# Tables of 32 channels built in place by two chains of VectorE operations, and the inverse's first step placed beside the taps

## The chip, the cores and the metric

The kernel runs on one core of a Trainium2 chip. It uses TensorE (PE in the profile, its weight loads are PEld), VectorE (DVE), ScalarE (ACT), very little of GpSimd (POOL), and SyncE (SP), whose queue issues nearly all transfers. The metric is the device time of one execution in microseconds (us). Three runs of the kernel before gave 597.43, 596.15 and 597.5 us, with a median of 597.43 us. Every engine works through its own list of instructions strictly in order. An instruction that is not ready holds back everything behind it on its engine.

## The reference, cut to what matters

Two independent computations stand side by side in the output.

```python
# A: Fourier mixing, x is 2048 x 512
a = einsum("bsd,ed->bse", x, dft_hid_re); b = einsum("bsd,ed->bse", x, dft_hid_im)
y_A = einsum("ts,bse->bte", dft_seq_re, a) - einsum("ts,bse->bte", dft_seq_im, b)

# B: S4D convolution, u is 2048 x 512, 128 modes for each of the 512 channels
dt = exp(log_dt); A = -exp(log_A_real) + 1j * A_imag; C = (C_real + 1j * C_imag) * dt[:, None]
K = 2.0 * einsum("dn,dnl->dl", C, exp((A * dt[:, None])[:, :, None] * arange(L))).real   # the taps
y_B = irfft(rfft(u_t, 2 * L) * rfft(K, 2 * L))[:, :, :L] + u * D_skip
return concatenate([y_A, y_B], axis=-1)
```

## The kernel before, in words

**Part A** (class `Fnet`) is a stream of 128x128 by 128x512 matrix products, line 273. Each factor is split into a high and a low part of the type fp32r, and each product is three matmuls: high by high, high by low, low by high. The split is done in `split` (lines 177 to 183): ACT rounds the high part (line 181) and DVE subtracts it (line 183). One item of the stream is one split tile, used by twelve matmuls. There are 160 items: 128 in the first eight groups (`s`) and 32 in the last four (`p`).

**Part B** (class `Ssm`) works on the 512 channels in 16 chunks of 32 channels (`CHUNK`). For every chunk it makes powers of a complex number, in which 2048 positions are written as 32 times 64. The seeds of a chunk are computed by `seed_args` (lines 532 to 536 on DVE, 528 to 546 on ACT) and multiplied into `cs` by `seeds` (line 556). From `cs` two tables are built by doubling. Table t1 has 32 columns per channel and table t2 has 64. A doubling is `mul` (line 482, into the scratch tiles `prod` or `prod2`), followed by `add` (line 491), which sums the halves of the scratch tile into the table. The even columns of t2 come from squares: `square` on ACT (line 500), `even_im` (line 508) and `even_re` (line 514) on DVE.

In the kernel before, the first columns of both tables are made for the 32 channels of a chunk at once in `base1` and `base2`. Then, for each half chunk of 16 channels, ACT copies the base into a fresh pair of tables t1 and t2 (`base_copy`, lines 652 and 654), and DVE makes the last two doublings for these 16 channels. The order in which the loop in `tables` (lines 607 to 648) yields its operations alternates between the two tables. There are three buffers of t1 and three of t2, each for 16 channels.

`taps` (lines 672 to 691) multiplies t1 by t2 on PE for two half chunks in one visit of 128 small matmuls (line 685), into one of the two slots `f` of PSUM. Each slot is two banks. `banks(n)` hands out n slots, and requests are served in the order in which they come. Two visits of taps give 64 channels, and `stage1_k` (line 705) starts their Fourier transform. Four quarters of 128 channels then go through `product` (lines 815 to 879): PE brings both spectra to frequency (line 826), ACT copies them out (line 839), four DVE operations multiply them (lines 842 to 855), and PE takes the first step of the inverse (line 862), which needs both slots. `inverse` (lines 890 to 911) loads the result back from memory and does the last step (line 901), ACT copies it out (line 906) and SP stores it (line 910).

**The order of the work** is made before launch, by the class `Plan` in the kernel file. Every piece of work is a generator that asks for an engine with a duration and an urgency. The planner takes, for the engine that comes free, the request that can start first and, among equals, the one with the smallest urgency number. The durations are formulas, such as 62 cycles plus one cycle per column for a DVE operation (`dve`, line 147). The matmuls of the stream have urgency 5, and all PE work of part B has urgency 1, so on PE the stream fills what part B leaves free. On DVE a split has urgency 0 while fewer than three items are ready ahead of the matmuls, the products of part B have 1 and the tables 2. What the planner decides is then the fixed order of each engine's list. If an engine is later on the chip than the planner thought, the order does not change and the others wait.

## Time and profile before

| what | value |
|---|---|
| median of three runs | 597.43 us |
| the profiled execution's own time | 599.18 us |
| its span, first to last instruction | 597.4 us |
| PE busy | 586.1 us (98%) |
| DVE busy | 504.7 us (84%) |
| ACT busy | 408.7 us (68%) |
| DMA queues, share of 16 engines | 69.3% |
| granted TensorE clock | 0.999 |

Busy time is the union of the instructions of an engine. Idle time in a row of the profile is the time that the engine stood still just before the instructions of that row, and the name behind the arrow is what ended most of it. The timeline lists instructions by engine with start, duration and shape; "x2" means that two like instructions were merged into one row. For PE it is best to compare starts: the end of a matmul is modelled, and consecutive matmuls overlap in the rows.

### The profile page before, as it was taken

How to read it: one execution, taken by the hardware profiler on the slowest of the kernel's cores; microseconds unless marked ns; L12 is line 12 of the kernel's file. 1: busy time of each engine (PE TensorE's matmuls, PEld its weight loads, DVE VectorE, ACT ScalarE, POOL GpSimd, SP SyncE). 2: the span in 40 equal slices, each digit the busy share in tenths (PEclk: the TensorE clock that was granted, in tenths of full speed). 3: DMA queues.
4: the chain of work that ended last, by engine and by line, in shares of the span. 5: the costliest groups of instructions: out<-in, count | busy, mean ns of one | idle time of the engine just before them, and what ended most of it. 6: DMA issues, size and time to landing. Idle time of an engine off the chain costs nothing.

```text
span 597.4 us, 17145 instructions
## 1 busy us (share of the span) xinstructions
PE 586.1 (98%) x6982; PEld 448.1 (75%) x6982; DVE 504.7 (84%) x993; ACT 408.7 (68%) x824; POOL 3.0 (0%) x12
## 2 busy tenths in 40 slices
PE   8999999999999999999999999999999999999997
PEld 6866666787867777887877877877778777787775
DVE  6999899989999999999999998999999996125540
ACT  5658898867767769677786686687867854344633
POOL 0000000000000000000000000000000000000000
PEclk9999999999999999999999999999999999999999
DMA  7998978472677656754856864568669637799756
GB/s 269 279 357 307 319 268 286 135 205 73 166 212 199 182 129 191 222 174 109 251 168 177 229 187 125 177 174 275 198 192 268 212 108 234 212 268 293 232 140 232
DMA packets 140991, 125.98 MB, mean 211 GB/s; under 512 B 46192, under 2 KB 105840, under 8 KB 140656
## 3 DMA queue, kind: packets, MB, share of 16 engines
q1 hardware_dynamic: 140912, 124.88, 69.3%
q8 instruction: 55, 0.90, 0.6%
q14 instruction: 24, 0.20, 0.1%
HBM read 82.12 MB, written 42.73 MB: 209 GB/s over the span
## 4 chain that ended last, share of the span: by engine, by line
PE 51%; DVE 25%; ACT 8%; DMA 7%; issue 7%; SPq 2%; DVEq 0%; ACTq 0%
PE acc L273 38%; DVE prod L482 7%; DVE lo L183 5%; DVE t L491 3%; PE f L826 3%; DMA par<-par_dram 3%; PE f L685 3%; PE f L901 2%; DMA raw<-in_sT 2%; PE f L862 2%; DVE base L491 2%; PE f L705 2%; ACT L540 2%; ACT hi L181 1%; DMA zl<-zs 1%
## 5 line engine op out<-in xcount | busy, mean ns | idle before, releaser
L273 PE MATMUL acc<-hi,x_hi 128*128 128x512 f32 x640 | 258.3, 404 | 0.5 <-ACT hi L181 0.3
L273 PE MATMUL acc<-lo,x_hi 128*128 128x512 f32 x640 | 250.8, 392 | 3.4 <-DVE lo L183 3.3
L273 PE MATMUL acc<-hi,x_lo 128*128 128x512 f32 x640 | 249.6, 390 | 0.0
L273 PEld LDWEIGHTS acc<-hi,x_hi 128*128 128x128 f32 x640 | 120.1, 188 | 49.7 <-issue 23.0
L183 DVE TENSOR_TENSOR lo<-raw,hi 128x512 fp32r<-128x512 f32 x160 | 109.6, 686 | 47.4 <-ACT hi L181 38.1
L273 PEld LDWEIGHTS acc<-lo,x_hi 128*128 128x128 f32 x640 | 120.2, 188 | 29.6 <-DVE lo L183 7.2
L273 PEld LDWEIGHTS acc<-hi,x_lo 128*128 128x128 f32 x640 | 120.2, 188 | 25.7
L181 ACT ACTIVATE hi<-raw 128x512 fp32r<-128x512 f32 x160 | 99.7, 626 | 58.0 <-PE acc L273 50.3
L482 DVE TENSOR_TENSOR prod<-base,cs 128x512 f32<-128x512 f32 (+3 forms) x160 | 88.9, 588 | 11.1 <-ACT base L593 9.2
L482 DVE TENSOR_TENSOR prod<-t,cs 128x1024 f32<-128x1024 f32 x64 | 78.1, 1221 | 0.8
L491 DVE TENSOR_TENSOR t<-prod 128x512 f32<-128x512 f32 (+1 forms) x128 | 68.1, 552 | 0.0
L287 ACT ACTIVATE y<-acc 128x512 f32<-128x512 f32 x48 | 28.3, 595 | 15.1 <-PE acc L273 13.0
L839 ACT ACTIVATE uk<-f 128x1024 f32<-128x1024 f32 x32 | 32.2, 1016 | 5.4 <-PE f L826 5.4
L685 PEld LDWEIGHTS f<-t,t 128*32 128x32 f32 x2048 | 29.5, 110 | 6.4 <-issue 3.5
L685 PE MATMUL f<-t,t 128*32 128x64 f32 x2048 | 32.3, 220 | 0.4 <-DVE t L491 0.4
L491 DVE TENSOR_TENSOR base<-prod 128x64 f32<-128x64 f32 (+2 forms) x96 | 28.8, 337 | 0.0
L842 DVE TENSOR_TENSOR z<-uk 128x512 f32<-128x512 f32 x32 | 22.0, 687 | 7.4 <-ACT uk L839 7.4
L500 ACT ACTIVATE prod<-t 128x512 f32<-128x512 f32 x32 | 20.1, 627 | 11.8 <-DVE t L491 11.7
L586 ACT ACTIVATE cs<-cs 128x352 f32<-128x352 f32 x32 | 15.3, 527 | 15.8 <-DVE cs L556 15.8
L500 ACT ACTIVATE square<-base 128x256 f32<-128x256 f32 x48 | 19.6, 408 | 5.2 <-DVE base L491 5.2
L714 ACT ACTIVATE xk_sb<-f 128x512 f32<-128x512 f32 x32 | 17.6, 595 | 7.8 <-PE f L705 7.8
L869 ACT ACTIVATE z<-f 128x512 f32<-128x512 f32 x32 | 17.7, 590 | 7.4 <-PE f L862 7.4
(90 smaller groups left out, 552.8 us busy)
## 6 DMA issues: line engine op xcount, KB each, us to landing
raw<-in_sT SPq DMA_DIRECT2D x128, 256.0 KB, 3.3
p<-y SPq DMA_DIRECT2D x32, 256.0 KB, 4.0
xt_u<-xu SPq DMA_DIRECT2D x32, 256.0 KB, 5.1
xk<-xk_sb SPq DMA_DIRECT2D x32, 256.0 KB, 3.9
xt_k<-xk SPq DMA_DIRECT2D x32, 256.0 KB, 5.3
zs<-z SPq DMA_DIRECT2D x32, 256.0 KB, 3.8
zl<-zs SPq DMA_DIRECT2D x16, 512.0 KB, 5.1
raw<-p SPq DMA_DIRECT2D x32, 256.0 KB, 3.7
```

Source lines behind the costliest of these rows:

```text
L181: self.nc.scalar.activation(hi, src, AF.Copy)
L183: self.nc.vector.tensor_tensor(lo, src, hi.bitcast(F32), op=OP.subtract)
L273: nc.tensor.matmul(acc[d], l[:, cols], r, start=k == 0 and n == 0, stop=k == len(items) - 1 and n == 2)
L287: self.nc.scalar.activation(y, ps, AF.Copy, scale=-1.0 if g[2] == 1 else 1.0)
L482: self.nc.vector.tensor_tensor(p.rearrange("p k d c m -> p k (d c) m"), src.rearrange("p d c l -> p (d c) l")[:, None, :, rows].to_broadca ...
L491: self.nc.vector.tensor_tensor(dst[:, :, :, rows], p[:, 0], p[:, 1, :, ::-1], op=OP.add)
L500: self.nc.scalar.activation(sq, t[:, :, :, m // 2:m], AF.Square)
L685: nc.tensor.matmul(ps[32 * j:32 * j + 32, 4 * o + i], t1[:, 4 * i + j, c], t2[:, 4 * i + j, c], start=c == 0, stop=c == 1, tile_position=( ...
L826: nc.tensor.matmul(got[r][1][32 * xx:32 * xx + 32, g, o:o + PART], self.w2[rows, 2 * q + r, xx, 32 * c:32 * c + 32], xt[rows, r, xx], star ...
L839: a.activation(uk[:, r].rearrange("p g n c d -> p g (n c d)"), p, AF.Copy)
L842: v.tensor_tensor(P[:, r], t[:, r], u[:, r], op=OP.mult)
L869: a.activation(z[:, :, 2 * n:2 * n + 2].rearrange("p r x d -> p x r d"), p[:, :, :2 * PART].rearrange("p x (r d) -> p x r d", r=2), AF.Copy)
```

## The change

In part B the two tables of a chunk are made for all 32 channels in their final tiles. There is no base tile and no copy by ACT. `tables` now only makes the seeds, in two buffers of `cs`. Two new generators consume them: `tables2` builds t2 (urgency 2, scratch `prod2`, one buffer of t2), and `tables1` builds t1 (urgency 2.2, scratch `prod`, two buffers of t1). Only the last doubling is still done in two halves of 16 channels, because of the size of the scratch tile.

`taps` now takes one chunk from one pair of tables and writes it to columns 256 to 511 of the two banks of a slot. The first step of the inverse in `product` writes only columns 0 to 255 of each bank. As long as taps are left to do, a product that has come this far waits in a list (class `Joined`). The next visit of taps takes it along: it asks for two slots instead of one, issues the inverse's 32 matmuls and then its own 128, and the first slot is given back when both have been copied out. A product that finds no taps left goes alone, as before.

Three smaller edits go along. At the start, the first 128 columns of the first tile of x are loaded and split on their own (`load_x0`), the first tile of the moving factor is loaded by ACT's queue instead of SP's, and the three warming matmuls have 216 columns instead of 256. At the end, the last of the inverse's steps is copied out in two halves by ACT and DVE and stored by two queues.

```diff
     def load(self, src, to, where, key, ev):
         raw = self.pool.tile([128, DM], F32, name="raw", bufs=RAWS)
-        yield "dma", load(256)
-        self.nc.sync.dma_start(raw, src)
+        if key == self.items[self.groups[0]][0]:
+            yield "act", 0.45
+            self.nc.scalar.dma_start(raw, src)
+            yield "dma2", load(256)
+        else:
+            yield "dma", load(256)
+            self.nc.sync.dma_start(raw, src)
...
+    def load_x0(self, raw):
+        yield "dma", load(64)
+        self.nc.sync.dma_start(raw[:, :128], self.xin[0, :, :128])
+        self.x[0] = self.still(0)
+        yield "act", act(128)
+        self.nc.scalar.activation(self.x[0][0][:, :128], raw[:, :128], AF.Copy)
+        yield "dve", dve(128)
+        self.nc.vector.tensor_tensor(self.x[0][1][:, :128], raw[:, :128], self.x[0][0][:, :128].bitcast(F32),
+                                     op=OP.subtract)
+        self.plan.set(self.x0_ev)
...
+class Joined(Event):
+    def __init__(self, ssm, run):
+        super().__init__()
+        self.ssm, self.fn, self.got = ssm, run, None
+    def run(self, got, shared=True):
+        self.got, self.users = got, {k: 1 for k, _ in got}
+        if shared:
+            self.users[got[0][0]] = 2
+        self.fn(got)
+    def leave(self, k):
+        self.users[k] -= 1
+        if not self.users[k]:
+            self.ssm.give(k)
...
+    def halves(self, name, t, rows, seed, to):
+        for d in (slice(0, CHUNK // 2), slice(CHUNK // 2, CHUNK)):
+            p = yield from self.mul(name, t[:, d], rows, seed[:, :, d])
+            yield from self.add(p, t[:, d], to)
+
+    def tables1(self):
+        for n in range(16):
+            yield self.t1s
+            yield self.cs_ev[n]
+            cs = self.cs[n]
+            t = self.tab.tile([128, CHUNK, 2, 32], F32, name="t1", bufs=2)
...
+            for j in range(4):
+                p = yield from self.mul("prod", t, slice(0, 2 ** j), cs[:, :, 6 + j])
+                yield from self.add(p, t, slice(2 ** j, 2 * 2 ** j))
+            yield from self.halves("prod", t, slice(0, 16), cs[:, :, 10], slice(16, 32))
...
+    def tables2(self):
+        for n in range(16):
+            yield self.cs_ev[n]
+            yield self.t2s
+            cs, t = self.cs[n], self.t2
...
+            p = yield from self.mul("prod2", t, slice(1, 2), cs[:, :, 1])
+            yield from self.add(p, t, slice(3, 4))
+            p = yield from self.mul("prod2", t, slice(1, 4), cs[:, :, 2])
+            yield from self.add(p, t, slice(5, 8))
+            for m in (8, 16):
+                ev, box = Event(), []
+                self.plan.spawn(self.square(t, m, ev, box), 0)
+                p = yield from self.mul("prod2", t, slice(1, m, 2), cs[:, :, 3 if m == 8 else 4])
+                yield from self.even_im(t, m)
+                yield from self.even_re(t, m, ev, box)
+                yield from self.add(p, t, slice(m + 1, 2 * m, 2))
+            yield from self.even_im(t, 32)
+            for d in (slice(0, CHUNK // 2), slice(CHUNK // 2, CHUNK)):
+                ev, box = Event(), []
+                self.plan.spawn(self.square(t[:, d], 32, ev, box), 0)
+                p = yield from self.mul("prod2", t[:, d], slice(1, 32, 2), cs[:, :, 5, d])
+                yield from self.even_re(t[:, d], 32, ev, box)
+                yield from self.add(p, t[:, d], slice(33, 64, 2))
...
+    def taps(self, ks, n, done):
+        yield self.t1_ev[n]
+        yield self.t2_ev[n]
+        other = self.waiting.pop(0) if self.waiting else None
+        got = yield from self.banks(2 if other else 1)
+        k, p = got[0]
+        yield "pe", 1.78 + (0.87 if other else 0)
+        if other:
+            other.run(got)
...
+        self.plan.put(self.t1s)
+        self.plan.put(self.t2s)
...
     def product(self, b, h, q, got, done):
...
+        w = Joined(self, run)
+        if self.taps_left:
+            self.waiting.append(w)
+            yield w
+        if w.got is None:
+            got = yield from self.banks(2)
+            yield "pe", 0.95
+            w.run(got, False)
         self.plan.put(b.uks)
...
     def inverse(self, b, h, i, n):
...
+        if h == 3 and n * (i + 1) == 32:
+            queue = nc.sync, nc.scalar
+            yield "act", act(256)
+            nc.scalar.activation(z[:, 0:2], ps[:, 0, :2 * PART].rearrange("p (w d) -> p w d", w=2), AF.Copy)
+            yield "dve", dve(256)
+            nc.vector.tensor_copy(z[:, 2:4], ps[:, 0, 2 * PART:].rearrange("p (w d) -> p w d", w=2))
+            for w in range(2):
+                queue[w].dma_start(self.out[:, o + 2 * w:o + 2 * w + 2, PART * h:PART * h + PART],
+                                   z[:, 2 * w:2 * w + 2])
+            return
```

The loops before, in `tables` and `seeds`, alternated between the tables like this:

```python
            p = yield from self.mul("prod", b1[:, d], slice(0, 8), cs[:, :, 9, d], 16)
            q = yield from self.mul("prod2", b2[:, d], slice(1, 16, 2), cs[:, :, 4, d], 16)
            ...
            yield from self.add(p, t1, slice(8, 16))
            yield from self.even_im(b2[:, d], 16, t2)
            yield copied
            p = yield from self.mul("prod", t1, slice(0, 16), cs[:, :, 10, d], 16)
            yield from self.even_re(t2, 16, ev, box)
            yield from self.add(q, t2, slice(17, 32, 2))
```

More of the change, by code (lines that the diff above doesn't have):

```diff
@@ L473, in load_par, with mul @@
         self.nc.sync.dma_start(self.par[ck], self.par_dram[:, :, o:o + CHUNK])
-    def mul(self, name, src, rows, seed, nd):
+    def mul(self, name, src, rows, seed):
+        nd = src.shape[1]
         m = len(range(64)[rows])
         n = 4 * nd * m
-        p = self.tab.tile([128, PROD[name]], F32, name=name)[:, :n].rearrange(
-            "p (k d c m) -> p k d c m", k=2, d=nd, c=2)
+        p = self.tab.tile([128, 1024], F32, name=name)[:, :n].rearrange("p (k d c m) -> p k d c m", k=2, d=nd, c=2)
         yield "dve", dve(n)
@@ L684, in taps @@
                     for j in range(4):
-                        nc.tensor.matmul(ps[32 * j:32 * j + 32, 4 * o + i], t1[:, 4 * i + j, c], t2[:, 4 * i + j, c],
+                        d = 16 * o + 4 * i + j
+                        nc.tensor.matmul(ps[32 * j:32 * j + 32, i], t1[:, d, c], t2[:, d, c],
                                          start=c == 0, stop=c == 1, tile_position=(0, 32 * j))
-            self.plan.put(self.ts)
-        yield "act", act(512)
-        nc.scalar.activation(ks[:, 4 * (g % 4):4 * (g % 4) + 8], ps, AF.Copy)
-        self.give(k)
+        self.plan.put(self.t1s)
+        self.plan.put(self.t2s)
+        self.taps_left -= 1
+        if other:
+            self.plan.set(other)
+        while self.waiting and not self.taps_left:
+            self.plan.set(self.waiting.pop(0))
+        yield "act", act(512)
+        nc.scalar.activation(ks[:, 8 * (n % 2):8 * (n % 2) + 8].rearrange("p (o i) l -> p o (i l)", o=2),
+                             p[:, :, 256:], AF.Copy)
+        if other:
+            other.leave(k)
+        else:
+            self.give(k)
         done()
@@ L855, in product, with run @@
         v.tensor_tensor(t[:, :, :, 0], t[:, :, :, 0], t[:, :, :, 1], op=OP.add)
-        got = yield from self.banks(2)
-        yield "pe", 0.95
-        for c, Y in enumerate((u, t)):
-            for g in range(2):
-                for xx in range(4):
-                    rows = slice(32 * xx, 32 * xx + 32)
-                    nc.tensor.matmul(got[xx // 2][1][64 * g:64 * g + 64, xx % 2, :2 * PART], self.ia[rows, c],
-                                     Y[rows, :, g, 0], start=c == 0, stop=c == 1, tile_position=(32 * xx, 64 * g))
+        def run(got):
+            for c, Y in enumerate((u, t)):
+                for g in range(2):
+                    for xx in range(4):
+                        rows = slice(32 * xx, 32 * xx + 32)
+                        nc.tensor.matmul(got[xx // 2][1][64 * g:64 * g + 64, xx % 2, :2 * PART], self.ia[rows, c],
+                                         Y[rows, :, g, 0], start=c == 0, stop=c == 1, tile_position=(32 * xx, 64 * g))
+        w = Joined(self, run)
[6 more added lines that the diff above has]
+            w.run(got, False)
         self.plan.put(b.uks)
@@ L916 @@
 BATCH = 2
-PROD = {"prod": 1024, "prod2": 512}
 def program(tc, i, o, parts="AB"):
```

194 lines of the change are left out of this document (73 added, 121 removed).

## The prediction

> **What bounds the kernel now.** I read the busy times first, then the busy times of the middle stage, then the groups of instructions, the waits, and stretches of the timeline. The first row is from the page, the second is the stretch from 60 to 500 us, with the engines in the same order.
>
> ```profile
> PE 586.1 (98%) x6982; PEld 448.1 (75%) x6982; DVE 504.7 (84%) x993; ACT 408.7 (68%) x824; POOL 3.0 (0%) x12
> 60.00:500.00 440.00, 436.26 (x5553) 334.36 (x5551) 419.91 (x833) 328.70 (x681) 2.51 (x7) 1.00 0.65 193
> ```
>
> PE is busy 586 of 597 us at full clock, so the time is the sum of PE's work and its holes. While the tables are made (up to about 500 us) DVE is busy too, 419.9 of 440 us. Two engines are full at once, and their orders are written beforehand. The next rows show how tightly they are coupled: taps on PE (L685), the last `add` of their tables on DVE (L491), and a split that came late (L183). The last row is from the waits: total, times, longest.
>
> ```profile
> 165.39 0.50 PE L273 MATMUL acc<-hi,x_hi 128*128 128x512 f32 x1
> 167.22 0.50 PE L273 MATMUL acc<-lo,x_hi 128*128 128x512 f32 x1 [1.33 <-DVE lo L183]
> ...
> 470.60 2.00 PE L685 MATMUL f<-t,t 128*32 128x64 f32 x128
> 470.72 0.69 DVE L491 TENSOR_TENSOR t<-prod 128x512 f32<-128x512 f32 x1
> ...
> 499.46 0.68 DVE L491 TENSOR_TENSOR t<-prod 128x512 f32<-128x512 f32 x1
> 500.14 1.99 PE L685 MATMUL f<-t,t 128*32 128x64 f32 x128
> ...
> PE acc L273 <- DVE lo L183: 3.3, 4, 1.3
> ```
>
> The last table is finished at 499.46 + 0.68 = 500.14, the moment its taps begin. At 470.60 the second table is finished (471.41) only while PE works on the first. Waits of PE for DVE add up to little (last row), but PE has no reserve here against a later DVE. And at 165.39 the next matmul came 1.83 us later instead of 0.23, for a split behind table operations. Whatever delays DVE in this stage, beyond what the planner allowed for, turns into holes on PE.
>
> **The change, part by part.** *Fewer DVE operations.* A doubling over 32 channels replaces two over 16.
>
> ```profile
> L482 DVE TENSOR_TENSOR prod<-t,cs 128x1024 f32<-128x1024 f32 x64 | 78.1, 1221 | 0.8
> L482 DVE TENSOR_TENSOR prod<-base,cs 128x512 f32<-128x512 f32 x96 | 63.0, 687 | 0.9
> L652 ACT ACTIVATE t<-base 128x256 f32<-128x256 f32 x32 | 13.1, 410 | 6.0 <-DVE base L491 6.0
> L654 ACT ACTIVATE t<-base 128x512 f32<-128x512 f32 x32 | 20.0, 625 | 3.2 <-DVE base L514 3.2
> DVE prod L482 <- ACT base L593: 9.2, 12, 1.2
> ```
>
> By the code a chunk has 14 `mul`, 14 `add`, 5 `even_im` and 5 `even_re` before, and 12, 12, 3 and 4 after: seven operations fewer, with the same columns. By durations, two of 687 ns against one of 1221 save 0.15 us. But neighbours overlap in the rows, so starts must be compared, and those come next.
>
> ```profile
> 313.13 1.23 DVE L482 TENSOR_TENSOR prod<-t,cs 128x1024 f32<-128x1024 f32 x1
> 314.28 0.68 DVE L183 TENSOR_TENSOR lo<-raw,hi 128x512 fp32r<-128x512 f32 x1
> ...
> 315.55 0.68 DVE L491 TENSOR_TENSOR t<-prod 128x512 f32<-128x512 f32 x1
> 316.15 0.89 DVE L556 TENSOR_TENSOR cs<-seed 128x704 f32<-128x704 f32 x1
> ...
> 333.56 0.68 DVE L491 TENSOR_TENSOR t<-prod 128x512 f32<-128x512 f32 x1
> 334.27 1.29 DVE L482 TENSOR_TENSOR prod<-base,cs 128x512 f32<-128x512 f32 x2
> ...
> 337.76 0.69 DVE L842 TENSOR_TENSOR z<-uk 128x512 f32<-128x512 f32 x1
> 338.48 0.69 DVE L844 TENSOR_TENSOR uk<-uk 128x512 f32<-128x512 f32 x1
> 339.09 0.68 DVE L842 TENSOR_TENSOR z<-uk 128x512 f32<-128x512 f32 x1
> ...
> 340.30 0.34 DVE L532 TENSOR_SCALAR seed<-seed 128x352 f32<-128x352 f32 x1
> 340.67 0.53 DVE L534 TENSOR_TENSOR seed<-seed 128x352 f32<-128x352 f32 x1
> ```
>
> A 1024-column operation takes 314.28 - 313.13 = 1.15 us of DVE, a 512-column one 316.15 - 315.55 = 0.60. Merging two saves 2 x 0.60 - 1.15 = 0.05 to 0.06 us; seven times 16 chunks make some 6 us of DVE. ACT loses L652 and L654, 33 us; ACT is 68% busy and not the engine that ends the waits above, so I count nothing. The 9.2 us of waits at the start of chunks (last row of the fence before) can go as well, since there the other chain can run.
>
> *Dependent neighbours.* The same fence has the price that matters most. L842 at 339.09 starts 0.61 us after an L844 that it has nothing to do with, but that L844 starts 0.72 us after the L842 whose input it overwrites. `add` takes 0.60 us up to an independent L556, and 0.71 up to a `mul` that reuses its scratch tile. L534 starts 0.03 us after the end of L532, whose result it reads, while independent operations start 0.08 before the end of the one in front. A neighbour that must wait for the one before it costs 0.11 us more.
>
> The loop before alternates between the tables, and by the code an operation follows the one it depends on at 6 places in a chunk. After the change each chain is a generator of its own. With urgencies 2 and 2.2 a free DVE always continues t2 as long as t2 can go on; t1 gets the time in which t2's buffer waits for its taps. So the chains do not alternate, and each runs in its own order: in t2 the operations 2, 3, 4, 5, 9, 13 and 17 of 19 follow directly on what they need, in t1 11 of 12. That is 18 places against 6. Splits and products come in between at some; I take 8 of 10 as left: 12 x 0.8 x 0.11 = 1.06 us a chunk, 17 us in 16 chunks. Bounds: 0 if other work separates all of them, 12 x 0.11 x 16 = 21 us if none.
>
> On DVE alone 17 - 6 - (0 to 9) leaves 2 to 11 us more until the tables are done. For PE it is worse, since the order is written with the planner's own prices. Its 62 cycles and one per column give 0.60 us for 512 columns: right for independent neighbours, without a term for dependent ones. What the planner knows of (seven operations, waits covered) it spends by placing the taps earlier among the matmuls; what it does not know, the 17 us, arrives as holes at L685 and at late splits. Against this stands a reserve that can be used once: at most three items of the stream are ready ahead, 12 matmuls of 0.23 us each, so 0 to 8 us. I take 4. Holes added: 17 - 4 = 13 us, between 0 and 21. Queued behind a waiting L685 are the stream's matmuls; behind those the buffers of hi and lo, and so ACT's next split.
>
> *The joint visit.* Entering and leaving the stream costs PE time.
>
> ```profile
> 572.73 0.39 PE L273 MATMUL acc<-hi,x_lo 128*128 128x512 f32 x1
> 573.04 1.12 PE L862 MATMUL f<-uk,ia 32*64 32x256 f32 x32
> 574.09 0.50 PE L273 MATMUL acc<-hi,x_hi 128*128 128x512 f32 x1
> 574.43 0.39 PE L273 MATMUL acc<-lo,x_hi 128*128 128x512 f32 x1
> ...
> 382.41 1.92 PE f L685 x128
> 384.33 1.90 PE f L901 x32
> ...
> L685 PE MATMUL f<-t,t x2048: 219/219/244, 73.5 to 501.9; 128*32 128x64 f32 x187
> L862 PE MATMUL f<-uk,ia x512: 374/374/426, 179.1 to 573.8; 32*64 32x256 f32 x171
> ```
>
> The last matmul before the visit holds 573.04 - 572.73 = 0.31 us and the first after it 574.43 - 574.09 = 0.34, where 0.23 is usual: 0.08 + 0.11 = 0.19 us saved when two visits become one. In the chain, two kinds of small matmuls stand directly behind each other (L685, L901) without a hole, so nothing is lost inside. The 16 visits of taps lie 28.4 us apart, from 73.5 to 500.1, and the first inverse step is at 179.1: by this average 12 visits follow it. One of them may be too early for the first product, so I take 11, and the last five products of 16 go alone. Gain 11 x 0.19 = 2.1 us, between 0 (products always just miss) and that. Waiting products hold the one `uk` buffer of their set, so the next product starts after the taps; they are four in a quarter and so are the taps, so they keep pace. A joint visit needs both slots; what waits behind it is other work of part B, while the stream covers PE.
>
> *Start and end.*
>
> ```profile
> 4.84 0.29 PEld L273 LDWEIGHTS acc<-hi,x_hi 128*128 128x128 f32 x1 [1.06 <-ACT hi L181]
> 13.99 0.19 PEld L273 LDWEIGHTS acc<-lo,x_hi 128*128 128x128 f32 x1 [0.40 <-DVE lo L183]
> 586.56 0.85 PEld L901 LDWEIGHTS f<-zl,ib 128*64 128x64 f32 x16 [0.35 <-issue]
> 593.36 0.60 ACT L287 ACTIVATE y<-acc 128x512 f32<-128x512 f32 x1 [0.34 <-PE acc L273]
> 593.99 0.34 SPq L295 DMA_DIRECT2D out_ya<-y  x1
> ```
>
> The first matmul waits for two splits on ACT of which the first shrinks to a quarter, and for a transfer that is issued 0.4 us sooner: up to 0.7 us. But at 14 us PE waits for a split of the fourth item anyway, so part of it returns as a hole. I take 0.4, between 0 and 0.7. The end is the stream's last y, which is not edited; if the inverse came last instead, half copies could save some 0.5 us. I take 0.
>
> *Without a price of its own:* the two memsets of t2 instead of the base, the warming matmuls, and the seeds. These are made a chunk ahead in two buffers; their load on SP's queue waits for the copy of the set before, which t1's chain issues at its start, a whole chunk of some 28 us ahead. Were it late, DVE would run dry, which is priced in the second rival.
>
> *Sum:* +13 - 2.1 - 0.4 = +10.5. From the span of 597.4 that is 608; the profiled execution's own time was 599.18, 0.3% above the median of 597.43, so I put the sum on the median: **608 us**.
>
> **The rivals.** *Faster.* The dependent neighbours do not reach PE, because other work separates them or the reserve swallows them. Then -2.1 - 0.4 and up to 3 us of the present holes, as DVE and ACT have less to do: 592 to 595, say 593.5. It decides this way below about 4 us of unplanned delay, the reserve. For it speaks that PE's holes before the split waits are few; against it the 0.11 us in three different lines and the zero reserve at 500.14. The Trainium skill, "VectorE: DVE Perf Modes", sections "The DRAIN you can't avoid" and "Rules for kernel authors", would have it so: it says a semaphore between chained operations costs nothing and that one should minimise the count of operations, not semaphores. The starts above disagree with it, 0.72 us against 0.61, and I follow the trace.
>
> *Much slower by the single t2.* The chain of t2 waits for the joint visit, which waits for two slots. If t1 has then no work left, DVE runs dry. A visit is 1.92 + 1.05 us (L685 in the chain, L862 from 573.04 to 574.09) and two copies of 0.6 us like L287's stand before it: some 4 us a chunk. It is covered by t1's 12 operations with 5952 columns, 7 us by the 1.15 and 0.60 us above. Uncovered in a quarter of the chunks it adds 15 to 18 us on top of 5 us of delay: about 618.
>
> *Late end.* The way from the last product (573.04) to the inverse's first matmul (586.56), 13.5 us, is covered by matmuls today; with the waiting products later, some of it shows: about 602.
>
> *The joining does nothing:* the sum loses 2.1 us and gives 610, inside the range.
>
> **How the numbers follow.** Differences within 0.3%, 1.8 us, cannot be told from no change. Forecast (holes of 6 to 20 us, 601 to 616) 0.50; single t2 0.08; late end 0.05; faster 0.30; a balance of gain and delay within 0.3% 0.07. Slower is 0.63. The range 592 to 616 reaches through the faster case; about one in ten lies above it and one below. The likeliest case alone has 601 to 616.
>
> **What would show it.** Right: DVE rows of `add` and `mul` in which each starts about 0.03 us after the end of the one before, some 14 a chunk; PE waits for `t L491` and `lo L183` of over 10 us in sum, where the waits for `lo` were 3.3; 31 table operations a chunk; L862 and L685 back to back in 11 visits; no L652 and L654. Wrong: t1 and t2 operations that alternate, or PE busy 99% with the tables done before 490 us.

## The result and the profile after

The median is 619.70 us against 597.43 before, a ratio of 1.0374 (95% interval 1.0353 to 1.0395). The forecast of 608.0 had the direction and the mechanism, but the time lies 3.7 us above the range, and the loss is twice the one forecast: +22.3 us against +10.5. The profiled execution took 619.57 us and its span is 617.8, 20.4 more than the 597.4 before. All of the difference is in the span.

The first row is from the page of the changed kernel (busy time by engine), the others are stretches of it, with the engines in the same order, then granted clock, DMA share and GB/s.

```profile
PE 593.2 (96%) x6982; PEld 451.4 (73%) x6982; DVE 511.1 (83%) x883; ACT 380.9 (62%) x745; POOL 3.6 (1%) x12
```
```profile
60.00:500.00 440.00, 424.83 (x5503) 322.28 (x5504) 418.25 (x713) 289.70 (x582) 3.39 (x8) 1.00 0.64 187
500.00:560.00 60.00, 59.12 (x826) 45.00 (x808) 25.91 (x39) 27.49 (x42) 0.00 (x0) 1.00 0.88 260
```

From 60 to 500 us PE is busy 11.4 us less than before (436.26), and DVE, with 110 instructions fewer over the span, is still busy 418 of 440 us. ACT is busy 28 us less over the whole span (380.9 against 408.7), which did not shorten the time. From 500 to 560 us PE is full again. The next rows are the matmuls of the taps (L720, before L685) and of the inverse's last step (L954, before L901): count, durations in ns, first and last start. The third row is the inverse of the kernel before.

```profile
L720 PE MATMUL f<-t,t x2048: 219/219/243, 72.8 to 495.4; 128*32 128x64 f32 x187
L954 PE MATMUL f<-zl,ib x256: 272/273/323, 303.5 to 594.3; 128*64 128x128 f32 x128
```
```profile
L901 PE MATMUL f<-zl,ib x256: 272/273/323, 253.1 to 592.1; 128*64 128x128 f32 x128
```

The taps end 6.5 us sooner than before (495.4 against 501.9), the inverse 2.2 us later, and then PE still has some 19 us of nothing but stream (its last matmul ends at 613.8). So neither the tables nor the end sets the time. The stream does: matmuls that could have stood beside part B are left over, because PE stood still earlier. The waits of PE, and the one of ACT that grew most (total us, times, longest):

```profile
PE acc L294 <- DVE lo L183: 7.6, 9, 1.8
PE acc L294 <- ACT y L308: 2.4, 5, 0.7
...
PE f L750 <- issue: 1.4, 2, 0.8
PE f L720 <- DVE t L533: 1.3, 2, 0.9
...
PE f L954 <- ACT uk L884: 1.2, 2, 1.0
```
```profile
ACT square L540 <- DVE t L533: 35.3, 22, 4.4
```

Idle time undercounts these holes, because consecutive matmuls overlap in the rows. So I went through PE's rows of both traces and compared starts: each matmul of the stream with 0.227 us after the one in front, each visit of part B with the shortest of its kind. Delays above 0.13 us are summed here in us, by what the late one waited for.

| PE was late for | before | after |
|---|---|---|
| the low part of a split (DVE) | 4.4 | 9.4 |
| a bank that ACT had still to copy out, or a split's high part (ACT) | 0.5 | 3.5 |
| a table, inside a visit of taps | 0.8 | 2.6 |
| other visits of part B | 2.9 | 10.2 |
| half clock, and the first matmuls | 0.6 | 3.8 |
| sum | 9.3 | 29.5 |

The sum rose by 20.2 us, the span by 20.4: in size, and to within about 1 us, the holes are the whole loss. This is where they come from, on DVE (start, duration, in the changed kernel):

```profile
207.75 0.38 DVE L524 TENSOR_TENSOR prod<-t,cs 128x128 f32<-128x128 f32 x1
208.16 0.28 DVE L533 TENSOR_TENSOR t<-prod 128x64 f32<-128x64 f32 x1
208.54 0.56 DVE L524 TENSOR_TENSOR prod<-t,cs 128x384 f32<-128x384 f32 x1
209.14 0.36 DVE L533 TENSOR_TENSOR t<-prod 128x192 f32<-128x192 f32 x1
209.53 0.69 DVE L524 TENSOR_TENSOR prod<-t,cs 128x512 f32<-128x512 f32 x1
```

One chain alone: each starts 0.03 to 0.10 us after the end of the one before. Counting all pairs on DVE whose second starts 0.028 to 0.040 us after the end of the first, there are 130 before and 274 after. Independent neighbours start 0.084 us before the end of the one in front, so a dependent pair costs 0.0344 + 0.0836 = 0.118 us, and 144 more of them make 17.0 us.

This count leaves out a second class. Another 17 pairs of table operations start about 0.10 us after the end of the one before (the third row above is one: a `mul` of 384 columns behind an `add` of 64), and the kernel before has none of them. By the same reckoning they cost 0.19 us each, 3.2 us more. So the trace has 20 us of added delay on DVE. That this meets the 20.2 us of holes so closely is partly chance, since 3.2 us of the holes are matmuls at half rate. Why these pairs wait longer isn't shown.

### The profile page after: what moved, and what is told of

It reads as the page before. It is cut to its first block, busy times and chain, and to the rows that moved or that the text cites. A ratio compares the mean times of both kernels' runs of the same rounds, so it can differ in the third digit from the quotient of the medians.

```text
span 617.8 us, 16971 instructions
## 1 busy us (share of the span) xinstructions
PE 593.2 (96%) x6982; PEld 451.4 (73%) x6982; DVE 511.1 (83%) x883; ACT 380.9 (62%) x745; POOL 3.6 (1%) x12
## 4 chain that ended last, share of the span: by engine, by line
DVE 39%; PE 35%; issue 10%; DMA 8%; ACT 5%; SPq 1%; DVEq 0%; ACTq 0%
PE acc L294 26%; DVE prod L524 10%; DVE t L533 8%; DVE lo L183 8%; PE f L871 3%; DMA zl<-zs 2%; DVE t L553 2%; PE f L954 2%; PE f L720 2%; PE f L907 2%; DVE z L887 1%; DVE x_lo L183 1%; DVE t L547 1%; DVE cs L594 1%; DVE uk L889 1%
## 5 line engine op out<-in xcount | busy, mean ns | idle before, releaser
L524 DVE TENSOR_TENSOR prod<-t,cs 128x1024 f32<-128x1024 f32 (+3 forms) x192 | 167.2, 872 | 7.9 <-ACT t L662 2.3
L294 PEld LDWEIGHTS acc<-hi,x_hi 128*128 128x128 f32 x640 | 120.8, 189 | 51.0 <-issue 18.9
L294 PEld LDWEIGHTS acc<-lo,x_hi 128*128 128x128 f32 x640 | 120.9, 189 | 37.0 <-DVE lo L183 14.2
L533 DVE TENSOR_TENSOR t<-prod 128x512 f32<-128x512 f32 (+4 forms) x192 | 98.5, 515 | 3.5
L540 ACT ACTIVATE square<-t 128x256 f32<-128x256 f32 (+1 forms) x64 | 36.8, 575 | 43.9 <-DVE t L533 35.3
L308 ACT ACTIVATE y<-acc 128x512 f32<-128x512 f32 x48 | 28.7, 600 | 22.4 <-PE acc L294 19.9
L720 PEld LDWEIGHTS f<-t,t 128*32 128x32 f32 x2048 | 29.5, 110 | 8.6 <-issue 5.0
L720 PE MATMUL f<-t,t 128*32 128x64 f32 x2048 | 32.6, 220 | 2.0 <-DVE t L533 1.3
L553 DVE TENSOR_TENSOR t<-square 128x128 f32<-128x128 f32 (+1 forms) x64 | 24.8, 387 | 0.0
L871 PE MATMUL f<-xt_k,w 64*32 64x128 f32 x1024 | 22.9, 271 | 1.0 <-issue 1.0
L889 DVE TENSOR_TENSOR uk<-uk 128x512 f32<-128x512 f32 x32 | 22.1, 690 | 0.7
L547 DVE SCALAR_TENSOR_TENSOR t<-t 128x128 f32<-128x128 f32 (+2 forms) x48 | 22.3, 466 | 0.2
```

Of the source, the lines that this page charges most:

```text
L294: nc.tensor.matmul(acc[d], l[:, cols], r, start=k == 0 and n == 0, stop=k == len(items) - 1 and n == 2)
L308: self.nc.scalar.activation(y, ps, AF.Copy, scale=-1.0 if g[2] == 1 else 1.0)
L524: self.nc.vector.tensor_tensor(p.rearrange("p k d c m -> p k (d c) m"), src.rearrange("p d c l -> p (d c) l")[:, None, :, rows].to_broadca ...
L533: self.nc.vector.tensor_tensor(dst[:, :, :, rows], p[:, 0], p[:, 1, :, ::-1], op=OP.add)
L540: self.nc.scalar.activation(sq, t[:, :, :, m // 2:m], AF.Square)
L547: self.nc.vector.scalar_tensor_tensor(t[:, :, 1, m:2 * m:2], t[:, :, 0, m // 2:m], 2.0, t[:, :, 1, m // 2:m], op0=OP.mult, op1=OP.mult)
```

## Experiments

The theory is that the loss is dependent neighbours on DVE, which the written order doesn't allow for. The rivals are that the tables of 32 channels themselves are dearer (one buffer of t2, other sizes), that the joint visit holds back its neighbours, and that the edits at the start cost something instead of gaining. Each kernel computes the whole reference. Ratios are to the kernel before, measured beside it on the same chip (its medians there were 595.14 to 596.44 us). "Pairs" are the dependent neighbours on DVE of the first class, and "holes" the sum of the last table, uncertain by up to 1 us, both from the kernel's trace. Where the stream ends before part B, a second number gives PE's idle time behind the stream's last matmul. The last column is the last start of the inverse. The last kernel has no such figures, because its profiled execution took 603.82 us and the eleven others 594.78 to 599.75.

| kernel | median us | ratio (95%) | pairs | holes us | last inverse |
|---|---|---|---|---|---|
| before | 597.43 | | 130 | 9.3 | 592.1 |
| after | 619.70 | 1.0374 (1.0353 to 1.0395) | 274 | 29.5 | 594.3 |
| before, serial | 621.77 | 1.0446 (1.0413 to 1.0480) | 278 | 22.5 + 6.2 | 613.0 |
| before, priced | 603.36 | 1.0111 (1.0084 to 1.0139) | 134 | 9.0 + 4.7 | 597.6 |
| before, new start | 599.21 | 1.0040 (1.0021 to 1.0059) | 136 | 9.4 | 581.9 |
| after, alternating | 607.71 | 1.0203 (1.0168 to 1.0238) | 141 | 18.9 | 573.1 |
| after, priced | 615.72 | 1.0333 (1.0306 to 1.0360) | 271 | 16.0 + 10.9 | 609.5 |
| after, both ("mended") | 599.91 | 1.0057 (1.0039 to 1.0076) | 147 | 11.8 | 583.4 |
| after, not joined | 622.87 | 1.0445 (1.0409 to 1.0482) | 257 | 30.4 | 584.3 |
| after, old start | 620.11 | 1.0418 (1.0378 to 1.0458) | 279 | 34.2 | 598.4 |
| mended, old start | 601.05 | 1.0077 (1.0047 to 1.0106) | 153 | 13.6 | 585.2 |
| mended, not joined | 598.27 | 1.0024 (1.0008 to 1.0041) | 135 | 8.3 | 560.9 |
| mended, long warming | 600.64 | 1.0055 (1.0033 to 1.0076) | 147 | 14.2 | 585.7 |
| mended, t1 first | 641.31 | 1.0745 (1.0727 to 1.0763) | 118 | 10.3 + 33.8 | 634.8 |
| mended, tables alone | 597.76 | 1.0020 (1.0004 to 1.0035) | | | |

**The order of the operations alone, in the kernel before.** Tiles, sizes, buffers and count of operations stay as before; in `seeds` and `tables` the operations of t1 stand in one row and those of t2 behind them.

```diff
             p = yield from self.mul("prod", b1[:, d], slice(0, 8), cs[:, :, 9, d], 16)
-            q = yield from self.mul("prod2", b2[:, d], slice(1, 16, 2), cs[:, :, 4, d], 16)
-            ...
             yield from self.add(p, t1, slice(8, 16))
-            yield from self.even_im(b2[:, d], 16, t2)
             yield copied
             p = yield from self.mul("prod", t1, slice(0, 16), cs[:, :, 10, d], 16)
+            yield from self.add(p, t1, slice(16, 32))
+            ...
+            q = yield from self.mul("prod2", b2[:, d], slice(1, 16, 2), cs[:, :, 4, d], 16)
+            yield from self.even_im(b2[:, d], 16, t2)
```

> The kernel before with one edit: in each half chunk and in the seeds, the operations on t1 stand in one row and those on t2 in another, instead of alternating. Number, sizes and buffers of the operations are the same, and nothing else of the change is in. Theory A: dependent neighbours from 130 to 270 to 340, 16 to 24 us of delay, of which most reaches PE: 610 to 620 us. If dependence costs nothing: 597 to 600 us.

Measured: 621.77 us, a ratio of 1.0446. The stretch of DVE and the longest wait of PE in this kernel:

```profile
306.45 0.27 DVE L491 TENSOR_TENSOR base<-prod 128x64 f32<-128x64 f32 x1
306.76 0.42 DVE L482 TENSOR_TENSOR prod<-base,cs 128x256 f32<-128x256 f32 x1
307.22 0.29 DVE L491 TENSOR_TENSOR base<-prod 128x128 f32<-128x128 f32 x1
307.55 0.69 DVE L482 TENSOR_TENSOR prod<-base,cs 128x512 f32<-128x512 f32 x1
```
```profile
PE f L898 <- DMA zl<-zs: 6.2, 1, 6.2
```

Each operation starts 0.03 to 0.04 us after the end of its neighbour, and the pairs rise from 130 to 278, as many as in the changed kernel (and 26 are of the second class). The loss is even larger, 26.6 us from the 595.14 beside it, in a kernel that has none of its tiles, joint visits or start. So the order is enough to cause such a loss. Its way is a little different: the tables end later here (last taps at 533.7), so that in the end the inverse waits 6.2 us for its own data.

**The other chain first, in the changed kernel.** The planner gets a mark for each DVE operation that would follow directly on the one of its own chain that it needs, and such a one stands back.

```diff
+    def held(self, p):
+        return p[4][0] == "dve" and self.last[0] is p and (self.last[1], getattr(p[4][1], "kind", None)) in AFTER
...
     def key(self, p):
         engine, _, *urgency = p[4]
-        return max(p[0], self.free.get(engine, 0.0)), urgency[0]() if urgency else p[1], p[2]
+        u = urgency[0]() if urgency else p[1]
+        return max(p[0], self.free.get(engine, 0.0)), u + 0.5 * self.held(p), p[2]
```

> The changed kernel with one edit in the planner: while one chain's next DVE operation would directly follow the one it depends on, another ready table operation goes first. Nothing is priced. Theory A: the dependent neighbours fall from 274 to 150 to 200, 9 to 14 us less unplanned delay, time 606 to 612 us. Theory B: 616 to 621 us, whatever the neighbours.

Measured: 607.71 us, 1.0203. On DVE (the editing of the planner moves L524 and L533 to L546 and L555):

```profile
204.80 0.38 DVE L546 TENSOR_TENSOR prod<-t,cs 128x128 f32<-128x128 f32 x1
205.10 0.40 DVE L555 TENSOR_TENSOR t<-prod 128x64 f32<-128x64 f32 x2
205.40 0.89 DVE L546 TENSOR_TENSOR prod<-t,cs 128x384 f32<-128x384 f32 x2
206.21 0.56 DVE L555 TENSOR_TENSOR t<-prod 128x192 f32<-128x192 f32 x2
```

The same operations now stand two and two ("x2": one of each chain, merged into a row), and each starts before the end of the one in front. The pairs fall from 274 to 141, by 15.7 us at 0.118 each, those of the second class from 17 to 7, by 2 us, and the span falls by 13.1 (617.8 to 604.7). Waits for the low part, by starts, fall from 9.4 to 0.9 us. What is left, 18.9 us of holes against 9.3 before, isn't added pairs: there are about as many as before.

**The planner told the price.** Alone, in the changed kernel and in the one before: the order may then change, but nothing makes the chains alternate.

```diff
+            if engine == "dve":
+                held = 0.115 * self.held(p)
+                self.last = p, getattr(dur, "kind", None)
+                dur = float(dur) + held
```

> The changed kernel with one edit, in the planner alone: a DVE operation of the tables, the seeds or the products that directly follows the one it depends on is planned 0.115 us longer. The operations are the same. Theory A (the delay that the planner does not know makes the holes on PE): as many DVE neighbours at +0.03 us as now (274), but the holes of PE over 0.13 us, 29.5 us in the changed kernel and 9.3 before, fall to 10 to 16 us, and the time from 619.7 to 603 to 608 us. Theory B (the single buffer of t2, or the joint visits, make the holes): 616 to 621 us, holes of 25 us and more. Theory C (the planner's prices for ACT are what is wrong): holes at y and uk stay, 612 to 618 us.

> The kernel before with only the planner's price of 0.115 us for a dependent neighbour; its 130 such neighbours make 15 us. If unplanned delay is what makes PE's holes also here: waits of PE for splits from 4.4 to under 2 us, time 592 to 596 us, unless the later tables uncover the end, then 597 to 603 us.

Measured: 615.72 us and 603.36 us. The changed kernel with the price, then the kernel before with it: waits of PE, and stretches from 60 to 500 us and at the end.

```profile
PE f L976 <- DMA zl<-zs: 8.7, 1, 8.7
...
PE acc L316 <- DVE lo L205: 1.0, 3, 0.4
```
```profile
60.00:500.00 440.00, 435.12 (x5386) 337.50 (x5386) 417.77 (x714) 295.96 (x591) 2.73 (x7) 1.00 0.64 193
...
560.00:614.40 54.40, 37.37 (x706) 28.24 (x704) 18.20 (x28) 19.64 (x31) 0.00 (x0) 0.87 0.71 216
```
```profile
PE f L923 <- DMA zl<-zs: 4.7, 2, 4.3
```
```profile
60.00:500.00 440.00, 437.21 (x5565) 336.67 (x5564) 412.39 (x814) 327.86 (x680) 3.68 (x7) 1.00 0.66 195
560.00:601.70 41.70, 31.73 (x491) 24.34 (x491) 10.35 (x16) 14.46 (x22) 0.00 (x0) 0.92 0.53 161
```

My expectation for the changed kernel was too good. The price does what it should in the middle: waits for the low part go from 7.6 to 1.0 us and PE is busy 435 of 440. But a planner that knows of the delay places the taps later (last start 520.8 against 495.4), the stream is used up before part B is, and at the end PE has 17 us in which it is not busy. The 17 us of DVE time are still there, and knowing of them only moves the loss from holes to the end. In the kernel before it is the same on a smaller scale: its 134 pairs, priced, cost 1.1%, for its end is uncovered too.

**Both.** 

> The changed kernel with both edits of the planner: chains alternate where a dependent neighbour would follow, and the dependent neighbours that are left are planned 0.115 us longer. Theory A: some 140 dependent neighbours are left as with alternation alone (141, 607.7 us); with their delay known, PE's holes of 28.7 us there fall to 12 to 18, and since the taps end 20 us earlier than in the priced version alone, the way from the last taps to the end is covered: 594 to 601 us. If the price only moves the loss to the end again, as it did without alternation (615.7 us): 606 to 610 us.

Measured: 599.91 us, 1.0057. Of the 22 us some 19 are back. (The 28.7 us of holes that the expectation gives for alternation alone are 18.9 by the table.) The rows are those of the changed kernel with both edits:

```profile
PE acc L316 <- DVE lo L205: 1.1, 3, 0.7
```
```profile
60.00:500.00 440.00, 435.94 (x5662) 336.85 (x5661) 416.23 (x729) 299.52 (x595) 3.78 (x8) 1.00 0.65 193
```

PE is busy as before the change (436.26). Between alternating and both, only the planner's knowledge differs, since the pairs are 141 and 147; yet the span falls by 7.4 us more and the holes by 7.1. In the kernel before, the same knowledge brought nothing (holes of 9.0 instead of 9.3 us beside the stream, and a longer time). My reading is that in the order of the changed kernel also those pairs turn into holes that the order before could carry. No run isolates that.

**The joint visit.** Without it, in the changed and in the mended kernel:

```diff
         w = Joined(self, run)
-        if self.taps_left:
-            self.waiting.append(w)
-            yield w
         if w.got is None:
```

> The changed kernel with the joining undone: every product takes its first inverse step alone, with two slots, as soon as it can. Visits of PE to part B 11 more, 2.1 us by 0.19 us each. Theory A: 620 to 623 us, the holes for the tables stay. Theory B (joint visits that wait for two slots, and hold them until three copies are done, make the holes before L750 and L954, some 6 us): 613 to 617 us.

> The alternating and priced version of the changed kernel (599.9 us, 62 visits of PE to part B) without the joining. 10 or 11 visits more, at 0.19 us each: 601.5 to 602.5 us if nothing else changes; under 599 us if waiting for taps and for two slots costs part B more than the visits save.

Measured: 622.87 us, 1.0445, and 598.27 us, 1.0024. The joint visit works as it was read. It was seen 11 times, and the rows of the first one (changed kernel) have no hole between the inverse's 32 matmuls and the 128 of the taps:

```profile
196.36 0.39 PE L294 MATMUL acc<-hi,x_lo 128*128 128x512 f32 x1
196.68 1.12 PE L907 MATMUL f<-uk,ia 32*64 32x256 f32 x32
197.73 1.99 PE L720 MATMUL f<-t,t 128*32 128x64 f32 x128
199.65 0.50 PE L294 MATMUL acc<-hi,x_hi 128*128 128x512 f32 x1
```

In the changed kernel the joining gains 0.7% (1.0374 against 1.0445, intervals apart). In the mended one the run without it is 0.3% faster by the medians, but the intervals overlap a little (from 1.0039, and up to 1.0041). What it does to part B can be seen in the inverse of the mended kernel, first with the joint visits, then without:

```profile
L976 PE MATMUL f<-zl,ib x256: 272/273/323, 304.1 to 583.4; 128*64 128x128 f32 x128
```
```profile
L973 PE MATMUL f<-zl,ib x256: 272/273/323, 272.5 to 560.9; 128*64 128x128 f32 x128
```

As products wait for the next taps, the inverse's first matmuls start 32 us later and its last 22. So a small fixed gain at the stream's edge stands against a later inverse. That the later inverse costs time isn't shown: in both mended kernels the stream's matmuls end last, at 593.4 and 592.7 us.

**The start.** Three runs with the edits at the start undone or done alone, and one with the long warming matmuls only.

```diff
-                        self.plan.spawn(self.load_x0(x_raw[:, 0]), -1)
...
-            self.nc.scalar.dma_start(raw, src)
+            self.nc.sync.dma_start(raw, src)
...
-            self.nc.tensor.matmul(ps[:, :216], z[:, :128], z[:, 256:472], start=n == 0, stop=n == 2)
+            self.nc.tensor.matmul(ps[:, :256], z[:, :128], z[:, 256:], start=n == 0, stop=n == 2)
```

> The changed kernel with the three edits at the start undone (first tile of x whole, first moving tile on SP's queue, warming with 256 columns). The first matmul starts at 4.85 us instead of 5.35, and the eight or so matmuls at 0.43 us behind it are gone: 2 to 2.5 us less, 617 to 618 us. If the late start is made up for by later holes in any case: 619 to 620 us.

> The same as the alternating and priced version, with the three edits at the start undone. If the later first matmul and its half clock (2 us in sum) reach the end once the rest has no holes that swallow them: 1 to 2.5 us less than that version. If the start is made up for by holes of the stream that come in any case, as the undone start alone suggested (620.1 against 619.7): the same within 1 us.

> The kernel before with only the three edits at the start. The prediction had them as 0.4 us of gain, between 0 and 0.7. By the changed kernel's trace the first matmul comes 0.5 us later (ACT copies the rest of x's first tile ahead of the moving tile) and the eight behind it run at 0.43 us: 1.5 to 2.5 us slower than before, 597.5 to 599 us on this run's 596.2. If the stream's later holes swallow the start: 595.5 to 597 us.

> The alternating and priced version with the three warming matmuls back at 256 columns and the other two edits of the start kept. With 216 columns every trace so far has the first eight or so matmuls of the stream at 0.43 us, with 256 two of five have not. If the short warming is the reason: matmuls at 0.23 us from the start and up to 2 us less, 598 to 599 us; else 599.5 to 601 us.

Measured: 620.11, 601.05, 599.21 and 600.64 us. The old start gains nothing in either version of the changed kernel (1.0418 against 1.0374 and 1.0077 against 1.0057, intervals overlap), and the long warming nothing by itself. In the kernel before, the new start costs 0.4% (1.0021 to 1.0059). The first rows of ACT and PE in the changed kernel, then of ACT in the one before:

```profile
3.46 0.31 ACT L217 ACTIVATE x_hi<-uk 128x128 fp32r<-128x128 f32 x1 [0.99 <-DMA uk<-in_x]
4.25 0.52 ACT L181 ACTIVATE x_hi<-uk 128x384 fp32r<-128x384 f32 x1 [0.48 <-DMA uk<-in_x]
4.68 0.61 ACT L181 ACTIVATE hi<-raw 128x512 fp32r<-128x512 f32 x1
```
```profile
5.35 0.79 PE L294 MATMUL acc<-hi,x_hi 128*128 128x512 f32 x1 [1.24 <-ACT hi L181]
6.07 0.80 PE L294 MATMUL acc<-lo,x_hi 128*128 128x512 f32 x1
6.67 0.63 PE L294 MATMUL acc<-hi,x_lo 128*128 128x512 f32 x1
7.09 0.63 PE L294 MATMUL acc<-hi,x_hi 128*128 128x512 f32 x1
```
```profile
3.50 0.63 ACT L181 ACTIVATE x_hi<-uk 128x512 fp32r<-128x512 f32 x1 [1.49 <-DMA uk<-in_x]
4.16 0.63 ACT L181 ACTIVATE hi<-raw 128x512 fp32r<-128x512 f32 x1
```

The split of the small first transfer starts at 3.46 us instead of 3.50, which is no gain to speak of. But in ACT's list the rest of x (128x384, which waits for its own transfer until 4.25) now stands ahead of the moving tile, so that this is split 0.52 us later and the first matmul starts at 5.35 instead of 4.85.

**One t2 buffer.** No run has two buffers of t2; one takes 32 x 2 x 64 values of 4 bytes, 16 KB of each partition. Instead, the urgencies are exchanged, so that t1 is built first and t2, with its single buffer, comes second.

```diff
-        self.plan.spawn(self.tables2(), 2)
-        self.plan.spawn(self.tables1(), 2.2)
+        self.plan.spawn(self.tables2(), 2.2)
+        self.plan.spawn(self.tables1(), 2)
```

> The alternating and priced version with the urgencies of the two chains exchanged, so that t1 goes first. If the single buffer of t2 were what paces the tables, giving t2's chain the second place would delay the taps and cost 3 us or more: above 603 us. If only the dependent neighbours count: 598 to 602 us with the same number of them (147).

Measured: 641.31 us, 1.0745. The stretches of this kernel, and a wait of DVE's table operations:

```profile
60.00:500.00 440.00, 434.79 (x5072) 339.61 (x5075) 380.73 (x675) 288.27 (x573) 1.82 (x7) 1.00 0.62 187
560.00:640.00 80.00, 41.18 (x842) 30.04 (x840) 19.62 (x30) 22.02 (x35) 0.00 (x0) 0.73 0.67 192
```
```profile
DVE prod L546 <- ACT t L664: 13.2, 5, 4.1
```

DVE runs dry: it is busy 380.7 of 440 us, 35 less than with t2 first (416.2). The tables end some 66 us later (last taps at 550.1 against 484.0), and after 560 us PE is busy only half the time. This fits a single buffer of t2 that limits the tables as soon as t2 doesn't come first. It is not shown to be that buffer alone, since `cs` and t1 have only two buffers each, and the exchange changes when they come free as well. In the changed kernel as it was made no such limit can be seen: DVE's gaps of more than 0.04 us between 60 and 500 us make 13.8 us, against 16.7 before.

**The tables alone, mended.** Neither joint visits nor the new start, but alternating chains and the price.

> Of the change only the tables of 32 channels by two chains are left (and the end's half copies), with the planner alternating and pricing; joining and start edits are undone. Not joined with the new start was 598.3 us against 596.4 before. If the start's edits cost there what they cost the kernel before (2.8 us): 595 to 597 us, equal to the kernel before or a little better, so that the tables themselves are free once their neighbours do not depend on each other. If the start is swallowed, as in the changed kernel: 598 to 600 us, and the tables themselves cost some 2 us.

Measured: 597.76 us against 596.21, 1.0020 (1.0004 to 1.0035). This was to tell apart whether tables of 32 channels are worth something once their order is right. The time lies between the two ranges expected, so it doesn't tell what the start costs here. A gain isn't seen: 33 us fewer of ACT's copies and seven DVE operations a chunk fewer leave the time where it was, within 0.35%. One reservation: the price is part of this run, and it cost the kernel before 1.1%, so a gain of the tables that it takes back isn't excluded. No version is faster than the kernel before.

## Why the prediction was wrong in size

*Dependent neighbours: right.* I counted 12 x 0.8 = 9.6 more a chunk at 0.11 us, 17 us. The trace has 144 more in 16 chunks, 9 a chunk, at 0.118 us: 17.0. The other signs came as told, 31 table operations a chunk, no L652 and L654 and 11 joint visits without a hole, but not quite the waits: those for the low part and for tables make 12.0 us by starts, but only 8.9 as idle time, the measure of the 3.3 before, and the sign was over 10. None of the signs against it came: the chains do not alternate, PE is busy 96%, and the last table is finished at 490.2, not before 490.

*The step that failed: "Holes added: 17 - 4 = 13 us".* This term was too small: the holes added were 20.2 us. Both of its parts were off. The 17 prices every neighbour at 0.11 us and leaves out the 17 pairs that cost 0.19 us, 3.2 us more. The 4, a reserve of items that are ready ahead, isn't seen in the time. In the kernel before with the serial order, 22 us of added delay (148 pairs at 0.118 and 26 at 0.19) became 20.9 us of span by the two traces (26.6 by the medians), and in the changed kernel 20 us became 20.4. Against it stands that alternating took away 17.6 us of delay and gave back only 13.1 us of span, which is near the 13 of the sum by luck: another 7.4 us came back only when the planner was told of the 141 pairs that remain, and the same knowledge gave nothing in the kernel before. The sum had nothing for such pairs, as if the old ones stayed harmless in any order. How the missing 7 us divide between the long pairs, the reserve, the old pairs and the clock (below) stays open. The 20.2 lie inside the bound of 21, but that bound stood for the added pairs alone.

I also sought the holes only at L685 and at late splits, in the first and third rows of the table of holes, where 6.8 us were added. As much again, 7.3, arose in other visits of part B, and 3.0 where the stream waits for ACT. My reading is that a late DVE also holds ACT. ACT's list has `square` in it, which waits for the tables, and the copies behind it come late for PE. The 35.3 us in 22 waits shown above stand against two rows in the kernel before:

```profile
ACT prod L500 <- DVE t L491: 11.7, 12, 2.5
```

The second has 5.2 us, for the squares of the base. The chain is read from the waits. No run isolates it, and against it speaks that alternating alone left 39.2 us of such waits with fewer holes.

*Clock: not in the sum.* 3.2 us of the added holes are matmuls at half rate, about half of them at the start; the last section has them. The sum put this at nothing.

*The joint visit, "-2.1 us"*: between the runs with and without it lie 0.7% of 597, 4 us with an uncertainty of more than 2. PE's visits to part B fell from 71 to 63, and eight times 0.19 us is 1.5. The size was about right here, but "they keep pace" was not: in the mended kernel the products' wait for taps puts the inverse's last matmuls 22 us later, and no gain in time is seen.

*The start, "-0.4"*: wrong in sign, by the run on the kernel before (0.4% slower). I priced the split that shrinks and did not look at what stands behind it in ACT's list, the rest of x with a transfer of its own. In the changed kernel this doesn't show in the time.

*The end, 0*: right in the changed kernel, where some 19 us of stream follow the last inverse.

*The rivals.* Faster, at 593.5: fell. It stood on the reserve swallowing the delay. By the Trainium skill's "VectorE: DVE Perf Modes" (sections "The DRAIN you can't avoid" and "Rules for kernel authors") a semaphore between chained operations costs nothing and the count of operations is what to reduce. These runs disagree: with the same operations in another order, the kernel before went from 595.14 to 621.77 us. Single t2: not in this order. The exchange of urgencies shows that the tables can become the limit, without telling t2's buffer from the others. Late end: not in the changed kernel, where the stream covers it, but it is where the loss went when the planner knew of the delay and the chains did not alternate. Its price of 602 was for another cause. Joining without effect: fell in the changed kernel (0.7%); in the mended one an effect isn't shown.

## What to carry to other kernels

Two chains that feed one in-order engine are worth interleaving by hand or by rule: as generators with fixed priorities, each runs through by itself, and every operation waits out the one before it. A planner that doesn't know this cost turns it into holes on the engine that is the bound. One that knows it, but cannot avoid it, moved the loss to the end here. Before pricing a moved step at a gain, read what stands behind it in the same engine's list.

## What was unexpected of the hardware

A short hole can cost the clock. In the changed kernel PE waits for a split, and the matmuls after the hole follow at 0.43 us instead of 0.23. The first rows have start, duration and PE; the last is the stretch behind the hole, in which the granted clock (third number from the right) is 0.53:

```profile
484.64 0.40 PE L294 MATMUL acc<-hi,x_hi 128*128 128x512 f32 x1
486.86 0.71 PE L294 MATMUL acc<-lo,x_hi 128*128 128x512 f32 x1 [1.82 <-DVE lo L183]
487.36 0.63 PE L294 MATMUL acc<-hi,x_lo 128*128 128x512 f32 x1
487.79 0.63 PE L294 MATMUL acc<-hi,x_hi 128*128 128x512 f32 x1
486.80:490.40 3.60, 3.54 (x9) 2.80 (x10) 3.37 (x6) 0.60 (x1) 0.00 (x0) 0.53 0.51 114
```

Eight late matmuls after this hole make 1.7 us, nearly as much as the hole itself. The Trainium skill, "TensorE: Matmul & The Clock Gate", section "Why this matters for your kernels", advises against gaps of over about 3 us. Here 1.82 us, about 1 us behind an earlier gap of 0.49, was enough. It isn't always: other gaps of 0.5 to 1.2 us after the start of the same trace, and one of 1.91 us in the kernel before with the serial order, have no such trail.

The same pace follows the first matmuls at 5.35 us above, where the kernel before had 0.23 us between starts from its third matmul on. The shorter warming is not the whole cause: with 216 columns it came in every trace, but with 256 in five of seven. What decides it stays open.
